# A gated linear attention feeding a squared-ReLU MLP: the instruction order planned anew, with other gates on the input transfers

## The chip, the cores and the metric

The kernel runs on one core of a Trainium2 chip. The metric is the device time of one execution in microseconds (us). Before the change the median of three runs is 176.64 us (176.60, 176.64, 176.91).

The engines have short names in the profile: PE multiplies matrices (PEld loads its stationary operand), DVE, ACT and POOL work on elements, SP issues transfers and does nothing else here. POOL issues transfers too. Each engine takes its own instructions strictly in order; engines wait for each other through semaphores.

## The reference

For each of 4 batches and 8 heads, a state of 48x48 runs over 768 tokens; the outputs of all heads of a token, 384 numbers, are a row x of a two-layer MLP:

```python
for t in range(S):
    state = alpha[:, :, t, :, None] * state + np.einsum('bhd,bhe->bhde', k[:, :, t], v[:, :, t])
    y[:, :, t] = np.einsum('bhd,bhde->bhe', q[:, :, t], state)
...
h = x @ w_in            # 384 -> 2048
r = np.maximum(h, 0.0)
return ((r * r) @ w_out).astype(np.float32)   # 2048 -> 384
```

Inputs and output are float32; 3072 rows of 384 come out.

## The kernel before

**Tiles.** The 3072 tokens are cut into 12 pieces of 256 tokens, called pairs here (g = 0 to 11; each is two chunks of 128, and three pairs make a batch). Each pair goes through these steps:

- `loads` (L497): four transfers issued by SP, alpha, k, q and v of the pair, 384 KB each, into one of four raw buffers. All loads of all pairs are kept in one order.
- `decay` (L519), or `decay_half` (L558) for pairs 0 and 1, which does it in two halves X of four heads: ACT takes logarithms (lab), PE sums them (L534, L536; L573, L578 for halves), ACT exponentiates (asb), DVE multiplies q and k by the result (qks; L555, L587). `values` (L511) makes a bf16 copy of v (vbf): on POOL for pairs 0 and 1 (L515), else on ACT (L517).
- the transposes of qks into qkt: on PE with eviction by ACT and DVE for pairs 0 to 3 (`turned`, L606 and L611; `turned_half`, L638, L649, L652), by a transposing DMA on SP from pair 4 on (`turned_dma`, L618).
- `scores` (L654): 64-wide matmuls (L666), then DVE applies the causal mask out of PSUM (pm, L676).
- `carry` (L682): the state to hand on (L695, then DVE L710/L713 and POOL L715).
- `mixed` (L723): the attention output of the pair, transposed as the MLP needs it (L734), copied by ACT into xt (L773). For pairs 6 to 10 `mixed_back` (L781) makes it token-major instead (L804, L794), ACT copies it into yb (L818), and a transposing DMA on SP (L821) makes xt.
- `up` (L838): 8 units of 6 matmuls 128x256 (L847) into psH0 and psH1 in turn, ReLU on ACT (rr, L853), square on DVE (gt, L855).
- `down` (L867): for each chunk 4 pieces of 4 matmuls 128x384 (L874) into psO, ACT copies out (osb, L881), then a store (L831) by SP, or by POOL in two halves for pairs 6 to 10. The last chunk is done in two column halves (L893, L900).

**Weights.** w_in comes in five pieces and w_out in four (`weights`, L474). POOL issues these transfers, which also cast to bf16. `RUNS` (L466) says after which load each run of pieces may start: (1, 3, 5) is five pieces after alpha of pair 1, (1, 2, 4) four pieces after v of pair 1. `OPENS` (L467) makes alpha of pair 2 wait for piece 5, the first of w_out.

**What sets the order.** Nothing is issued in program order of the source. Each step is recorded with a number `at` (pair index times two plus an offset, L904 to L931), its cost and its dependences; `Program.order` (L88) then plays list scheduling with assumed durations, transfer rates (L39 to L43) and instruction-fetch blocks (L47), picks for each engine the ready step with the smallest `at`, and so fixes each engine's instruction order. `fill` (L263) puts matmuls on zeros into planned idle time of PE ahead of the first `down`; `busy` (L859) issues seven such matmuls of 512 columns at the start. Nobody reads their output. `plan` and `emit` turn dependences into semaphore waits. So a constant or an offset changes the order of whole engines.

Of the kernel before, what the change touches and what calls it, by code (L numbers as in the profile page):

```python
# [14 lines left out]

class Op:


    def __init__(self, n, eng, fn, work, at, dma=None, nbytes=0, rate=0.0):
        self.n, self.eng, self.fn, self.work, self.at = n, eng, fn, work, at  # L20
        self.dma, self.nbytes, self.rate = dma, nbytes, rate
        self.deps = {}
        self.users = []
        self.waits = []
        self.count = None
        self.signal = False
        self.form = None
        self.size, self.late = 0, 0.0


class Program:
# [7 lines left out]
    BEGIN = {"SP": 1200.0, "POOL": 2700.0}  # L39
    LANDING = {"SP": 900.0, "POOL": 1400.0}  # L40
    PAIR, ROWS, TURN = 325.0, 390.0, 135.0
    PACKET = {PAIR: 120.0, TURN: 256.0}
    LONG = 1792.0  # L43
    HOLD = 2500.0
    SWITCH, STICK = 95.0, 1.0

    BLOCK, AHEAD_OF_ALL, FETCH, CALM, BUSY_UNTIL = 256, 37, 5200.0, 500.0, 36000.0  # L47
    FILL, SHARE, WIDE = 215.0, 0.75, 4

    def __init__(self, nc):  # L50
        self.nc = nc
        self.ops = []
        self.writer = {}
        self.readers = {}
        self.slots = {}

    def add(self, eng, fn, work, at, reads=(), writes=(), dma=None, nbytes=0, rate=0.0, behind=None, form=None,
            drain=None, size=0):
        op = Op(len(self.ops), eng, fn, work, at, dma, nbytes, rate)
        for r in reads:  # L60
# [23 lines left out]
        op.form, op.size = form, size  # L84
# [3 lines left out]
    def order(self, until):  # L88
        until = {op.n for op in until}
        missing = {}  # L90
        for op in self.ops:
            missing[op.n] = len(op.deps)
            for d in op.deps:
                self.ops[d].users.append(op)
# [11 lines left out]
        def done(op, t, users):  # L106
            for u in users:
                known[u.n] = max(known[u.n], t)
                missing[u.n] -= 1
                if not missing[u.n]:  # L110
# [3 lines left out]
        now = [0.0]  # L114

        def transfer(limit):

            while now[0] < limit:
                on = [e for e in queue if queue[e] and queue[e][0][0] <= now[0]]
                end = min([limit] + [queue[e][0][0] for e in queue if queue[e] and e not in on])  # L120
                if not on:
                    if end == limit:
# [3 lines left out]
                    continue  # L126
                rate = {}
                for e in on:
                    op = queue[e][0][2]
                    rate[e] = op.rate if len(on) == 1 else self.PACKET.get(op.rate, self.LONG) / sum(  # L130
                        self.PACKET.get(queue[o][0][2].rate, self.LONG) / queue[o][0][2].rate for o in on)
# [7 lines left out]
                if queue[first][0][1] <= 1e-3:  # L139
                    op = queue[first].pop(0)[2]  # L140
                    op.landed = op.landed0 = end + self.LANDING[first]
# [10 lines left out]
        for op in self.ops:  # L152
            if not missing[op.n]:
# [5 lines left out]
        used, there, filling = self.AHEAD_OF_ALL, {}, True  # L159
        while left:  # L160
# [37 lines left out]
            op = self.ops[n]  # L198
            if e == "PE":
                if op.form != form:  # L200
                    op.work += self.SWITCH
                form = op.form
                filling = filling and n not in until
                if filling and used > self.AHEAD_OF_ALL:
                    gap = 2 * int(max(0.0, t - free[e]) * self.SHARE / self.FILL)
                    used, there = self.take(used, gap, free[e], 100.0, there)[:2]
                used, there, late = self.take(used, op.size + 1, t, op.work, there)
                op.work += late
                op.late = late
            free[e] = t + op.work  # L210
            op.start = t
            programs[e].append(op)
            self.sequence.append(op)
            left -= 1
            if op.dma is not None:
                if e == "SP":
                    issued += 1
                    if op.rate == self.TURN:
                        turning[0] = op
                queue[e].append([t + self.BEGIN[e], float(op.nbytes), op])  # L220
                done(op, free[e], [u for u in op.users if u.eng == e and u.deps[n] == "order"])
            else:
                end = free[e] + self.LATENCY[e]
                if e == "PE":
                    done(op, free[e], [u for u in op.users if u.eng == e and u.deps[n] != "drain"])
                    done(op, end, [u for u in op.users if u.eng == e and u.deps[n] == "drain"])
                else:
                    done(op, free[e], [u for u in op.users if u.eng == e and u.deps[n] == "war"])
                    done(op, end, [u for u in op.users if u.eng == e and u.deps[n] != "war"])
                reserve = self.RESERVE if op.at > 4 else 0  # L230
                done(op, end + reserve, [u for u in op.users if u.eng != e])
        self.programs = programs

    def take(self, used, size, t, work, there):
# [3 lines left out]
        block = used // self.BLOCK  # L238
        for b in range(block + 1, (used + size) // self.BLOCK + 1):
            at = t + late + work * (b * self.BLOCK - used) / size  # L240
            late += max(0.0, there.get(b, 0.0) - at)
            there[b + 1] = max(at, there.get(b, 0.0)) + self.FETCH - (self.CALM if at > self.BUSY_UNTIL else 0.0)
# [87 lines left out]
def bass_gla_recurrent__then__act_relu_squared_kernel(  # L330
# [71 lines left out]
    turn = [0]  # L402

    def bank():
        i = turn[0] % len(psG)
        turn[0] += 1
        return psG[i], ("psG", i)
# [50 lines left out]
    BACK = 6  # L458
    TURNED = 4
    SELF = 12  # L460


    RUNS = [(1, 3, 5), (1, 2, 4)]
    OPENS = {2: 5}
# [9 lines left out]
    def weights(at, run):  # L474
        x0 = sum(r[2] for r in RUNS[:run])
        w0, j0, n0 = RUNS[run]
# [21 lines left out]
    def loads(g, at):  # L498
        b, t0, r = g // NW, (g % NW) * TW, g % NRAW
        for j, src in ((3, alpha), (0, k), (1, q), (2, v)):  # L500
# [3 lines left out]
            eng = "SP" if g < SELF else "POOL"  # L504
            last_load[0] = add(eng, lambda e, s=s, dst=dst: e.dma_start(dst, s), 500 if g < SELF else 1000, at + 0.1 * (j != 3),
                               writes=raw(r, j), reads=gate, dma=("raw" if g < SELF else "own") + f"{r}_{j}",
                               nbytes=TW * HD * 4, rate=pr.PAIR, behind=last_load[0])
            if g - 2 in turns and j == 3:
                last_load[0].deps.setdefault(turns[g - 2].n, "order")

    def values(g, at):  # L511
        r, vb = g % NRAW, g % NV
        dst, src = VBF[vb][:, :, :, 0:D], both(r, 2)
        if g < FIRST:
            add("POOL", lambda e: e.tensor_copy(dst, src), 910, at, reads=raw(r, 2), writes=[("vbf", vb)])  # L515
# [3 lines left out]
    def decay(g, at):  # L519
# [4 lines left out]
        def product(dst, at_, a0, a1, reads, writes):  # L524
            add("DVE", lambda e: e.tensor_tensor(dst, a0, a1, ALU.mult), 470, at_, reads=reads, writes=writes)  # L525
# [13 lines left out]
        add("PE", sums, 265, at + 0.02, reads=lab + ["hinc"], writes=[key], size=2 + 2 * NP)  # L539
# [13 lines left out]
        for z in range(2):  # L553
# [4 lines left out]
                writes=[("qks", x, z, X) for X in range(2)])  # L558
        values(g, at + 0.3)

    def decay_half(g, X, at):

        r, l, a, x, c_ = g % NRAW, g % NLAB, g % NASB, g % NQK, g % NAC
        ps, key = bank()
# [5 lines left out]
        def sums(pe):  # L570
            for o in range(2):
                for i in range(2):
                    pe.matmul(ps[:, o * HH:(o + 1) * HH], (HEXC if i == 1 and o == 0 else HINC)[:],  # L573
                              LAB[l][:, i, hs, 0:D], start=i == 0, stop=i == 1)
            for j in range(2):
                for i in range(2):
                    h = 4 * X + 2 * j
                    last = pe.matmul(ps[:, HD + 2 * j:HD + 2 * j + 2],  # L578
                                     LAB[l][:, i, h:h + 2, :].rearrange("p a b -> p (a b)"),
                                     HINC[:, 63:128:64], start=i == 0, stop=i == 1)  # L580
            return last
        add("PE", sums, 430, at + 0.01, reads=[("lab", l, X), "hinc", "hexc"], writes=[key], size=16)
# [409 lines left out]
```

## Time and profile before

| what | value |
|---|---|
| median of three runs | 176.64 us |
| span of the profiled execution, first to last instruction | 175.4 us |
| the rest of a run, median less span | 1.2 us |
| PE, DVE, ACT, POOL busy | 169.2, 120.3, 115.4, 31.3 us |
| first `up` matmul starts | 19.07 us |
| first `up` matmul of pair 2 starts | 47.06 us |
| HBM read, written | 25.17 MB, 4.72 MB |

The profile is of one execution; its own time outside the span is not recorded, so 1.2 us is taken for it. The page gives busy times, the chain of work that ended last, the groups of instructions by source line and the transfers; the views of windows, waits and single tiles are answers of the same trace. L numbers are lines of the kernel before. Times inside the execution count from the first instruction.

### The profile page before, as it was taken

What the parts mean: (1) busy time and instruction counts of PE and PEld (TensorE: products, weight loads), DVE (VectorE), ACT (ScalarE), POOL (GpSimd) and SP (SyncE); (2) the same over time, 40 slices, a digit from 0 to 9 for tenths busy, and PEclk for the clock granted to TensorE, in tenths of its full rate; (3) what the DMA queues carried; (4) which work ended last, traced back from release to release, by engine and by line L of the source; (5) the groups of instructions that cost most, each with busy time, mean ns of one, the idle gap of its engine ahead of it and who ended that gap; (6) DMA issues with size and microseconds to landing.
All of it is one profiled execution on the core that took longest, in us unless ns stands there. A gap on an engine that the chain in (4) does not pass through costs nothing.

```text
span 175.4 us, 5998 instructions
## 1 busy us (share of the span) xinstructions
PE 169.2 (96%) x2614; PEld 123.4 (70%) x2614; DVE 120.3 (69%) x253; ACT 115.4 (66%) x235; POOL 31.3 (18%) x56
## 2 busy tenths in 40 slices
PE   7987999999999999999999999999999999999994
PEld 2554777775777678777776776776787777777773
DVE  7799643689989898957949749759749527322320
ACT  2763565895798598778749659658665563476541
POOL 4189110001011012010020010212222221220120
PEclk9999999999999999999999999999999999999999
DMA  5999999999997999998999996999639622202222
GB/s 143 325 298 174 204 203 251 255 317 308 331 244 145 273 222 262 216 265 267 117 319 191 185 327 113 176 331 124 122 76 78 135 49 45 49 0 49 47 45 90
DMA packets 77818, 32.30 MB, mean 184 GB/s; under 512 B 71264, under 2 KB 77472, under 8 KB 77792
## 3 DMA queue, kind: packets, MB, share of 16 engines
q1 hardware_dynamic: 72720, 26.81, 67.1%
q0 software_dynamic: 5072, 5.11, 16.9%
q8 instruction: 20, 0.33, 0.8%
q14 instruction: 6, 0.05, 0.1%
HBM read 25.17 MB, written 4.72 MB: 170 GB/s over the span
## 4 chain that ended last, share of the span: by engine, by line
PE 93%; DVE 4%; ACT 1%; issue 1%
PE psH L847 37%; PE psO L874 35%; PE psG L734 5%; PE psG L666 4%; PE psO L862 3%; DVE qks L587 3%; PE psG L695 2%; PE psO L893 2%; PE psG L804 1%; PE psG L606 1%; DVE pm L676 1%; PE psG L794 1%; PE psG L534 1%; PE psG L573 1%; ACT xt L773 1%
## 5 line engine op out<-in xcount | busy, mean ns | idle before, releaser
L853 ACT ACTIVATE rr<-psH 128x512 bf16<-128x512 f32 x96 | 57.0, 600 | 35.3 <-PE psH L847 34.2
L847 PE MATMUL psH<-xt,win 128*128 128x256 bf16 x576 | 75.3, 273 | 0.1
L874 PE MATMUL psO<-wout,gt 128*128 128x384 bf16 x368 | 73.3, 326 | 0.0
L855 DVE TENSOR_TENSOR gt<-rr 128x512 bf16<-128x512 bf16 x96 | 40.7, 428 | 40.8 <-ACT rr L853 40.4
L847 PEld LDWEIGHTS psH<-xt,win 128*128 128x128 bf16 x576 | 54.9, 98 | 13.7 <-ACT xt L773 0.4
L874 PEld LDWEIGHTS psO<-wout,gt 128*128 128x128 bf16 x368 | 34.2, 98 | 15.6
L676 DVE TENSOR_TENSOR pm<-psG,mask 128x512 bf16<-128x512 f32 x48 | 30.4, 681 | 0.7 <-PE psG L666 0.7
L715 POOL TENSOR_TENSOR sbf<-ust,acp 128x192 bf16<-128x192 f32 x16 | 10.0, 626 | 86.0 <-DVE ust L713 86.0
L555 DVE TENSOR_TENSOR qks<-raw,asb 128x768 bf16<-128x768 f32 x20 | 18.5, 952 | 0.8 <-ACT asb L544 0.8
L831 POOL DMA_DIRECT2D out_dram<-osb x20 | 10.8, 544 | 44.3 <-ACT osb L881 44.3
L881 ACT ACTIVATE osb<-psO 128x384 f32<-128x384 f32 x23 | 11.3, 490 | 5.0 <-PE psO L874 4.5
L525 DVE TENSOR_TENSOR raw<-raw 128x384 f32<-128x384 f32 x20 | 11.5, 581 | 0.0
L544 ACT ACTIVATE asb<-psG 128x384 bf16<-128x384 f32 x20 | 9.9, 493 | 0.5 <-PE psG L536 0.4
L773 ACT ACTIVATE xt<-psG 128x384 bf16<-128x384 f32 x14 | 7.6, 600 | 3.1 <-PE psG L734 3.1
L517 ACT ACTIVATE vbf<-raw 128x768 bf16<-128x768 f32 x10 | 8.6, 860 | 0.0
L862 PE MATMUL psO<-warm 128*128 128x512 bf16 x20 | 7.5, 498 | 1.1 <-DVE warm L420 1.1
L666 PEld LDWEIGHTS psG<-qkt 64*64 64x64 bf16 x384 | 5.9, 106 | 3.5 <-issue 1.9
L666 PE MATMUL psG<-qkt 64*64 64x128 bf16 x384 | 8.3, 219 | 0.0
L713 DVE TENSOR_TENSOR ust<-psG,sbf 128x192 f32<-128x192 f32 x15 | 5.3, 355 | 3.4 <-PE psG L695 1.7
L818 ACT ACTIVATE yb<-psG 128x384 bf16<-128x384 f32 x10 | 4.6, 489 | 3.9 <-PE psG L794 3.0
L734 PEld LDWEIGHTS psG<-pm,vbf 64*64 64x64 bf16 x336 | 4.9, 107 | 2.0 <-DVE pm L676 0.6
L530 ACT ACTIVATE lab<-raw 128x384 bf16<-128x384 f32 x10 | 5.3, 529 | 1.4 <-DVE raw L525 1.3
(71 smaller groups left out, 123.4 us busy)
## 6 DMA issues: line engine op xcount, KB each, us to landing
raw<-in_alpha_dram SPq DMA_DIRECT2D x12, 384.0 KB, 4.5
raw<-in_k_dram SPq DMA_DIRECT2D x12, 384.0 KB, 5.0
raw<-in_q_dram SPq DMA_DIRECT2D x12, 384.0 KB, 5.2
raw<-in_v_dram SPq DMA_DIRECT2D x12, 384.0 KB, 5.9
out_dram<-osb SPq DMA_DIRECT2D x13, 192.0 KB, 4.9
out_dram<-osb POOLq DMA_DIRECT2D x20, 96.0 KB, 2.3
wout<-in_moe_w_out_dram POOLq DMA_DIRECT2D x4, 384.0 KB, 11.8
win<-in_moe_w_in_dram POOLq DMA_DIRECT2D x3, 384.0 KB, 8.5
```

Of the source, the lines that this page charges most:

```text
L525: add("DVE", lambda e: e.tensor_tensor(dst, a0, a1, ALU.mult), 470, at_, reads=reads, writes=writes)
L555: add("DVE", lambda dve, z=z, decays=decays: dve.tensor_tensor(QKS[x][:, z, :, :, 0:D], both(r, z), decays, ALU.mult), 870, at + 0.05 + 0. ...
L666: last = pe.matmul(banks[i, j // 2][0][64 * c:64 * c + 64, col:col + 128].rearrange("p (a b) -> p a b", a=2), QKT[t][64 * i:64 * i + 64, 0 ...
L676: add("DVE", lambda dve, i=i, X=X, ps=ps: dve.tensor_tensor(PMB[m][:, i, 2 * X:2 * X + 2].rearrange("p j n s -> p j (n s)"), ps[:].rearran ...
L734: last = pe.matmul(o, lhsT, rhs, start=(c, n % 2) not in begun, stop=True, skip_group_check=True)
L831: add(by, lambda e, dst=dst, ps=ps: e.dma_start(dst, OSB[o][ps, :]), 600, at + 0.01 * i, reads=[("osb", o)], dma=("own" if by == "POOL" el ...
L847: last = pe.matmul(ps[:, f * TW:(f + 1) * TW].rearrange("p (c t) -> p c t", c=2), WIN[:, kt, fj * 128:(fj + 1) * 128], XT[:, 2 * (g % NX): ...
L853: add("ACT", lambda act: act.activation(RR[r][:], ps[:], AF.Relu), 480, at, reads=[key], writes=[key, ("rr", r)])
L855: add("DVE", lambda dve: dve.tensor_tensor(gt[:, 2 * u:2 * u + 2, :], rr, rr, ALU.mult), 340, at, reads=[("rr", r)], writes=[("gt", g % NG ...
L862: last = pe.matmul(psO[i % NPO][:, 0:128 * wide].rearrange("p (a b) -> p a b", a=wide), WARM[:], bass.AP(tensor=WARM, offset=0, ap=[[128, ...
L874: last = pe.matmul(ps[:, 0:DM], GT[g % NGT][:, fj, tt * 128:(tt + 1) * 128], WOUT[:, fj, :], start=(fj == 0), stop=(fj == FT - 1))
L881: add("ACT", lambda act: act.activation(OSB[o][:], ps[:, 0:DM], AF.Copy), 372, at, reads=[key], writes=[key, ("osb", o)])
```

## The change

The planner and its numbers are replaced; what is computed stays. In the built program:

- **Order.** A table with offsets for each pair and step replaces four shared rows of offsets, and the planner's assumptions on rates, fetch blocks (254 instructions for 256), the cold start of PE and the SBUF port shared by DVE and POOL change. Every engine's order changes. On PE, pair 0 now goes through scores, carry and the first 48 matmuls of `mixed` ahead of the transposes of pair 1; before, the transposes and half of the scores of pair 1 came first.
- **v of pairs 0 and 1.** The POOL copy also waits for all of that pair's qks.
- **Weights.** Eight pieces follow alpha of pair 1 and the ninth v of pair 1 (`PARTS`), so POOL's copy of v of pair 1 comes after eight pieces and the first state multiply, not after five.
- **Loads.** Alpha of pair 2 waits for piece 6 (second of w_out), alpha of pair 3 for piece 7. The loads of pairs 4 and 5 stand ahead of the first store in SP's queue. Only pairs 10 and 11 still wait for an earlier transpose to be issued (9 and 8); before, every pair from 6 on waited for that of two pairs earlier.
- **y by tokens** (`mixed_back`) for pairs 7 to 10; pair 6 goes by `mixed`, its rows stored by SP.
- **The sums** for the state (128x2 matmuls) of pairs 0 and 1 are all done with the second half: 4 and 12 matmuls for the halves, where 8 and 8 stood.
- **The start.** 14 matmuls of 256 columns for 7 of 512; later fillers write psO1 alone. In all 25 fillers for 20.
- **PSUM banks** go by least recent use, and pairs 0 and 1 may use psH and psO0 too.

```diff
-    RUNS = [(1, 3, 5), (1, 2, 4)]
-    OPENS = {2: 5}
+PARTS = ((1, 3, 8), (1, 2, 1))
+OPENS = {2: 6, 3: 7}
-    BACK = 6
+BACK = (7, 8, 9, 10)
+BEHIND = {10: 9, 11: 8}
+WARMUP = (14, 2)
...
-    BLOCK, AHEAD_OF_ALL, FETCH, CALM, BUSY_UNTIL = 256, 37, 5200.0, 500.0, 36000.0
+    BLOCK, AHEAD_OF_ALL, FETCH, CALM, BUSY_FROM, BUSY_UNTIL = 254, 56.0, 6500.0, 2000.0, 11200.0, 31000.0
...
+TABLE = [
+    dict(decay0=-98.35796, decay1=-86.77717, turned0=-92.08415, turned1=-74.82202, scores0=-76.59803, scores1=-74.23854, carry=-69.28206, mixed=-45.90118, up=-40.7555, down=13.8692, ...
...
-            if g - 2 in turns and j == 3:
-                last_load[0].deps.setdefault(turns[g - 2].n, "order")
+            if g in BEHIND and j == 3:
+                last_load[0].deps.setdefault(turns[BEHIND[g]].n, "order")
...
         if g < FIRST:
-            add("POOL", lambda e: e.tensor_copy(dst, src), 910, at, reads=raw(r, 2), writes=[("vbf", vb)])
+            add("POOL", lambda e: e.tensor_copy(dst, src), 830, at,
+                reads=raw(r, 2) + [("qks", g % NQK, z, X) for z in range(2) for X in range(2)], writes=[("vbf", vb)], port=True)
...
-            for j in range(2):
-                for i in range(2):
-                    h = 4 * X + 2 * j
-                    last = pe.matmul(ps[:, HD + 2 * j:HD + 2 * j + 2],
...
+            for j in range(2 * NP * X):
+                h, i = j // 2 * 2, j % 2
+                last = pe.matmul(ps[:, HD + h:HD + h + 2],
...
     def turned_back(g):
-        return BACK <= g < G - 1
+        return g in BACK
...
-    add("PE", lambda pe: busy(pe, 7, 4), 2950, -6, reads=["warm"], writes=[("psO", i) for i in range(NPO)], size=14)
+    add("PE", lambda pe: busy(pe, WARMUP[0], WARMUP[1]), 2950, -6, reads=["warm"], writes=[("psO", 1)], size=2 * WARMUP[0],
+        cold=False)
```

More of the change, by code (lines that the diff above doesn't have):

```diff
@@ L159, in order @@
         used, there, filling = self.AHEAD_OF_ALL, {}, True
+        port = {"DVE": 0.0, "POOL": 0.0}
+        other = {"DVE": "POOL", "POOL": "DVE"}
         while left:
@@ L197, in order @@
             n = pick[1]
[L198 to L209, printed above, removed]
@@ L699, in mm @@
             return last
-        add("PE", mm, 170 + 150 * len(chunks), at, reads=[("qks", x, 0, X) for X in range(2)] + [("vbf", vb)],
+        add("PE", mm, 250, at, reads=[("qks", x, 0, X) for X in range(2)] + [("vbf", vb)],
             writes=[b[1] for b in banks], form=64, size=32 * len(chunks))
```

385 lines of the change are left out of this document (272 added, 113 removed).

## Prediction

> **What bounds the kernel now.** I read the chain of waits first, then the busy time by stretch, then the timelines of the start, then the landing times. From the page and the stretches:
>
> ```profile
> PE 93%; DVE 4%; ACT 1%; issue 1%
> 27.14:47.06 19.92, 19.92 (x272) 14.38 (x270) 15.66 (x30) 14.13 (x31) 0.75 (x1) 1.00 1.10 293
> 47.06:110.00 62.94, 62.94 (x1083) 46.76 (x1081) 51.94 (x104) 49.31 (x103) 5.46 (x8) 1.00 1.01 226
> 110.00:173.00 63.00, 62.98 (x869) 47.25 (x867) 32.51 (x68) 36.36 (x70) 12.78 (x24) 1.00 0.51 94
> ```
>
> The columns are length of the stretch, then busy time of PE, PEld, DVE, ACT, POOL, the granted clock and the transfers. From 27.14 to 173 us PE is busy all the time: no wait there to remove. The change can win only ahead of 27.14, by less PE work, or not at all; it can lose anywhere. Two views of the start:
>
> ```profile
> 16.99 0.83 PE psG L734 x48
> 17.84 1.18 ACT xt L773 x2
> 19.07 1.48 PE psH L847 x12
> 26.65 0.65 PE psO L874 x4
> ```
>
> This is the chain: first `up` unit at 19.07, after the copies of xt, after `mixed` of pair 0.
>
> ```profile
> 8.07 0.82 POOL L515 CAST vbf<-raw 128x768 bf16<-128x768 f32 x1 [4.51 <-DMA raw<-in_v_dram]
> 9.41 4.00 POOL L481 DMA_DIRECT2D win<-in_moe_w_in_dram  x5 [0.53 <-DMA raw<-in_alpha_dram]
> 13.42 0.84 POOL L515 CAST vbf<-raw 128x768 bf16<-128x768 f32 x1
> 14.19 3.00 POOL L483 DMA_DIRECT2D wout<-in_moe_w_out_dram  x4
> 12.77 2.84 DVE L587 TENSOR_TENSOR qks<-raw,asb 128x384 bf16<-128x384 f32 x4
> ```
>
> A qks product takes 0.55 us, one following another every 0.47; but four took 2.84 us from 12.77 (one of them 1.44) and one at 8.12 took 1.18, each beside a POOL copy of v.
>
> The landing times, asked piece by piece: the last two pieces of w_in
>
> ```profile
> DMA to landing us min/median/max: 8.5/8.5/8.5
> DMA to landing us min/median/max: 9.6/9.6/9.6
> ```
>
> issued at 11.88 and 12.65, so landed at 20.4 and 22.2; the piece before landed at 18.45. w_out lands at 24.15, 26.2, 28.1 and 30.95. One piece takes 1.9 us in the stream; the last took 2.9 beside pair 2's loads, of which alpha is issued at 24.16, on the landing of piece 5.
>
> **The change, part by part.**
>
> 1. *Pair 0 first: the first `up` unit.* Alpha and k land as before, so the first qks product starts at 6.3 (before 6.42). The copy of v now waits for all four, so they run at 0.47: done 8.3 (before 9.30). Two qkt copies of 0.41 on DVE: 9.25. Four masks, one every 0.60 from 9.2: done 11.7 (before 12.86). Four products of pair 1, no copy beside them: 11.6 to 13.6 (before 12.77 to 15.61). `mixed` of pair 0 no longer stands behind pair 1's transposes: its 48 matmuls (0.70) at 11.75. The rest needs sbf (0.34 on DVE, 13.9), six matmuls (0.15), the second transposes (0.45), six more: ends 14.9. One xt copy of 0.60, the other chunk's was done early: **first `up` at 15.7**, 3.4 earlier.
>
> 2. *The weights hold it.* Piece 1 of w_in is needed at 15.7 (landed 13.7), the second at 16.4 (lands 16.55), the third lands at 18.45, the fourth at 20.4. POOL's first issue stays at 9.41, for alpha of pair 1 lands at 9.12 and the copy of v, started 8.4, ends 9.25. So units 0 and 1 are done with 0.75 us to spare, units 2 and 3 run 18.5 to 19.8, half of pair 1's scores 0.33, unit 4 waits for 20.4. From there: units 4 and 5 1.4, `mixed` of pair 1 0.95, unit 6 0.75, twelve matmuls 0.29, unit 7 0.65, one `down` 0.65: 25.1. Before, the same work was done at 27.14: **-2.05**. Of 3.4 won, 1.35 is lost to the weights.
>
> 3. *To the first `up` of pair 2 (47.06 before).* xt of pair 1 is copied by 25.1; eight units (5.24) and three `down` pieces (1.95): 32.4, each later than its w_out piece. Then twelve `down` pieces (7.8), pair 2's transposes, carry and scores, sums of pairs 2 and 3 and the changes of tile shape (2.7): `mixed` of pair 2 at 42.9 to 44.1. The new order has used up every `down` of pair 1 by then; before, one stood between `mixed` and this `up`, another inside `mixed`. What is late next: the sums of pair 3 (PE 41.9), two exps (0.49 each, a logarithm between them), two products of 0.95 end at 44.9, its transposes at 45.4; two xt copies of 0.60 behind 44.3 and ACT's other work end at 45.6. `up` at 45.7: **-1.36**, so 0.7 is given back.
>
> 4. *The rest.* Unit, piece and changes of shape are the same number (29 episodes of 64-wide work behind the first `up` in both orders). Pair 6 costs 0.70 + 0.27 + 0.29 by `mixed` (pair 3's row) for 0.85 by `mixed_back` (88.36 to 89.48 less a carry of 0.27): **+0.25**, for +0.4 at most. It saves SP one transpose of y.
>
> Costed at nothing: the 14 narrow matmuls (same 3584 columns, and the sums wait for ACT's logarithm at 4.90 anyway); the regrouped sums (0.1 earlier for the first half, 0.2 later for the second, inside the 0.75 of step 2); banks; planner numbers without effect on the order. If the 0.75 is used up, the start costs one for one.
>
> *POOL's copies, moved.* The copy of v of pair 0 now falls beside qkt copies and masks. Beside a mask, POOL's multiply at 17.18 (0.55) and the masks (0.68, as elsewhere) cost each other nothing; beside a qks product the copy cost 0.63. Between 0 and +0.63 I take 0, since the copies read PSUM as the masks do; the spare 0.75 covers the other end. The Trainium skill, "SBUF — State Buffer", section "Who interferes with whom", says that a DVE instruction with two SBUF inputs and a GpSimd one that reads SBUF exclude each other for a whole instruction, and that one with at most one SBUF input outside its two-port modes does not contend; by it the cost is 0 too. The 1.18 and 1.44 for 0.55 agree with its first half; no run yet shows a copy out of PSUM beside the cast.
>
> *Pair 2 let in late.* Its alpha is issued at 26.2 for 24.16. Its lateness is between 0 and 2.0. I take 0 for the last load: pieces 7 and 8 of the weights keep the queues full until then (DMA slices of 9), so alpha merely shares later, and v of pair 2 landed at 35.2 behind the same bytes. Alpha is then there at 31.4; its product, logarithm and sums are wanted at 34.4. The Trainium skill, "DMA: Bandwidth & Descriptors", in its part on software and hardware descriptor generation, says that an engine goes round-robin between the queues and changes at packet boundaries; by it a late alpha takes its share from the last piece alone, which ends near 31 as before. That piece's 2.9 us beside the loads agrees.
>
> *The DMA transposes.*
>
> ```profile
> DMA to landing us min/median/max: 4.2/5.5/6.1
> DMA to landing us min/median/max: 2.8/4.5/5.3
> ```
>
> The first line is for qkt, the second for xt. SP issues the first 3.0 to 4.6 us after PE's sums (48.38 to 52.99, 92.10 to 95.63). So scores need 7.2 to 10.7 us after the sums. With PE full from 45.7, I added up the new order by rows (a unit 0.655, a `down` piece 0.65, the rest as above): it leaves 15, 14, 11.3, 16, 16, 18, 11.3 and 12 us for pairs 4 to 11. Pair 6 is the tightest, 0.6 of room, since a store and a load of k stand ahead of it. For y of pairs 7 to 10 it leaves 8, 9, 6 and 6 us from ACT's copy, against up to 5.3, and more where a qkt transpose is still ahead in the queue. Taken as 0; between 0 and +1.
>
> **Sum**: 175.4 - 2.05 + 0.7 + 0.25 = 174.3 of span; with 1.2 outside it **175.5 us**, against the median 176.64.
>
> **Rivals.**
>
> - *Transposes late* (steps 4's cover fails at pair 6 and at y of 7 or 10): two waits of 0.4 to 0.6 each, 176.5. For: SP takes its list strictly in order, and five stores and loads now wait there between two transposes. Against: the room worked out above.
> - *Slower: the loads of pairs 2 and 3 shift by the whole 2.0 us.* Then alpha of pair 3 lands at 39.0 for 37.0. On DVE its product now stands between the two qkt copies of pair 2, and ACT's logarithm of pair 4's alpha between pair 3's two exps. PE has no `up` left to put in: scores of pair 2, due at 39.3, come at 40.3, and pair 3's transposes another 1.0 later. +2.0: 177.5. It decides once alpha of pair 3 lands after 38. Against it: bytes, not issue, set those landings before.
> - *It does not give back*: the transposes of pair 3 and xt of pair 2 are ready when PE is, at 45.0: 174.8; with w_out and w_in landing 0.4 earlier, because POOL issues eight pieces without a copy between, 174.4.
> - *The early start comes to nothing*: the copy of v of pair 0 and PSUM banks borrowed from psH and psO hold pair 0 past 0.75 of spare; 176.6, no change.
>
> **Chances.** Forecast 0.50 (own range 175.0 to 176.2), transposes late 0.17, loads late 0.15, no giving back 0.12, no early start 0.06. A measurement of this kernel can tell about 0.2% (0.35 us) from no change. Faster by more: 0.50 less 0.02, and 0.12, and 0.06 of the transposes' case: 0.66. Within: 0.16, mostly late transposes and no early start. Slower: 0.18 (late loads and the worse half of late transposes). The range takes in the case without giving back and the loads' case: 174.3 to 177.5; below lies what the weights forbid, above it several waits at once.
>
> **What will show it.** First `up` near 15.7, the fifth unit at 20.4 right behind the landing of its piece, the first `down` done at 25.1, `up` of pair 2 near 45.7, PE busy without a gap from there to the end, end of span at 174.3. No qks product of pairs 0 and 1 over 0.6 us. Wrong if weights land at other times than before, if scores of pair 2 or 3 wait on a load, or if scores of pair 6 or the first units of pairs 7 to 10 wait on SP's transposes.

## The result, and the profile after

The changed kernel is **slower** by 0.8%: 178.63 us (median of 11 runs, 177.39 to 180.03) against 177.07 for the kernel before (11 runs, 176.60 to 178.85). The ratio is 1.0084, with a 95% interval of 1.0057 to 1.0111. On another chip it was 1.0053 (1.0018 to 1.0087). The forecast was 175.5. The ratios here and below compare fast executions alone, and one can differ by up to 0.4% from the quotient of the two medians.

The profiled execution took 178.44 us with a span of 176.2, so 2.2 us lie outside the span. The executions of the changed order have 2.17 to 2.29 us there (all but one variant, the last experiment), those of the kernel before 1.68 to 1.81. The 1.2 us of the prediction was too small for either: it set the median of three executions, which with 1.75 us outside would have a span of 174.9, against the 175.4 of another execution. As a span 175.4 is usual: the medians on five chips are 174.9 to 175.5.

The shares of the chain that ended last:

```profile
PE 71%; DMA 13%; SPq 9%; POOL 3%; ACT 1%; DVE 1%; issue 1%; DVEq 0%
```

It was 93% PE before. Now PE comes into it only at 49.33 us; ahead of that it runs mostly through transfers and SP's issuing. The first `up` units, which the change brought forward, do not stand in it. Its middle part:

```profile
13.50 0.74 POOL wout L574
14.27 11.80 DMA wout<-in_moe_w_out_dram
...
40.37 1.15 SPq L595
41.56 6.35 DMA raw<-in_v_dram
```

The second piece of w_out lands at 26.08. Alpha of pair 2 waits for it by the new gate (a gate here is the wait of a load for a piece of the weights). Then come eleven issues of SP, one behind the other, and last the load of v of pair 4. The chain does not say that an earlier gate brings this load forward by as much: in the profile before, alpha of pair 2 was issued 1.93 us earlier, and v of pair 4 only 0.47 (41.09). Next three stretches, from the first `down` done, from the first `up` of pair 2 (both the same work as in the prediction's table) and from 110 us:

```profile
24.90:45.65 20.75, 20.13 (x272) 14.49 (x271) 15.43 (x29) 14.97 (x32) 0.76 (x1) 1.00 1.08 262
45.65:110.00 64.35, 62.74 (x1095) 46.91 (x1093) 51.78 (x104) 48.21 (x100) 4.92 (x8) 1.00 0.97 227
110.00:173.80 63.80, 63.78 (x870) 47.41 (x868) 32.27 (x68) 37.83 (x72) 10.96 (x20) 1.00 0.45 98
```

PE (second figure) was busy through all three before. Now the first lacks 0.6 us, the part that the prediction saw given back, and the middle one 1.6. The chain goes on there:

```profile
47.92 0.02 issue
47.94 0.84 ACT vbf L608
48.78 0.50 ACT rr L958
49.28 0.05 issue
49.33 1.49 PE psH L952 x12
```

The load of v of pair 4 lands at 47.92. ACT copies it (L608 of the changed kernel) and only then does the ReLU `rr` (L958) that frees psH for PE's third `up` unit of pair 2. The copy itself is wanted by nobody before `carry` of pair 4 at 58.6. ACT's timeline (start, duration, operation, idle time before it in brackets):

```profile
45.29 0.54 ACT L638 ACTIVATE ro<-ro 128x384 f32<-128x384 f32 x1
47.94 0.84 ACT L608 ACTIVATE vbf<-raw 128x768 bf16<-128x768 f32 x1 [2.11 <-DMA raw<-in_v_dram]
48.69 1.07 ACT L958 ACTIVATE rr<-psH 128x512 bf16<-128x512 f32 x2
```

The planner put the copy in line ahead of the ReLU; by its own times it would start at 46.0. In the kernel before, ACT does the first two ReLUs of pair 2 ahead of the copy:

```profile
47.92 1.25 ACT L853 ACTIVATE rr<-psH 128x512 bf16<-128x512 f32 x2
49.07 0.48 ACT L544 ACTIVATE asb<-psG 128x384 bf16<-128x384 f32 x1
49.44 0.84 ACT L517 ACTIVATE vbf<-raw 128x768 bf16<-128x768 f32 x1
```

DVE stands in the same way, under the cover of ACT's wait:

```profile
46.65 0.55 DVE L616 TENSOR_TENSOR raw<-raw,ro 128x384 f32<-128x384 f32 x1
49.06 0.56 DVE L616 TENSOR_TENSOR raw<-raw 128x384 f32<-128x384 f32 x1 [1.87 <-DMA raw<-in_alpha_dram]
49.54 0.75 DVE L960 TENSOR_TENSOR gt<-rr 128x512 bf16<-128x512 bf16 x2
```

This product belongs to pair 5, whose alpha lands at 49.04; behind it wait the squares gt of pair 2. In the kernel before, this product stands behind the fourth gt.

At the start all went as forecast in this execution. DVE and POOL:

```profile
6.81 1.50 DVE L680 TENSOR_TENSOR qks<-raw,asb 128x384 bf16<-128x384 f32 x3 [0.18 <-DMA raw<-in_q_dram]
8.33 0.42 DVE L745 COPY qkt<-psH 128x512 bf16<-128x512 bf16 x1
8.80 0.42 DVE L745 COPY qkt<-psG 128x512 bf16<-128x512 bf16 x1
9.16 0.69 DVE L769 TENSOR_TENSOR pm<-psG,mask 128x512 bf16<-128x512 f32 x1
```

```profile
8.38 0.82 POOL L605 CAST vbf<-raw 128x768 bf16<-128x768 f32 x1 [4.81 <-DVE qks L680]
```

Three products take 0.50 each; beside POOL's cast (8.38 to 9.20) two qkt copies take 0.42 each, as they do alone. The first mask starts at 9.16 and so hardly meets the cast.

### The profile page after: what moved, and what is told of

Its sections match the earlier page's. It is cut to its first block, busy times and chain, and to the rows that moved or that the text cites. A ratio compares the mean times of both kernels' runs of the same rounds, so it can differ in the third digit from the quotient of the medians.

```text
span 176.2 us, 6026 instructions
## 1 busy us (share of the span) xinstructions
PE 168.7 (96%) x2631; PEld 123.7 (70%) x2631; DVE 118.7 (67%) x253; ACT 116.8 (66%) x233; POOL 28.9 (16%) x52
## 4 chain that ended last, share of the span: by engine, by line
PE 71%; DMA 13%; SPq 9%; POOL 3%; ACT 1%; DVE 1%; issue 1%; DVEq 0%
PE psH L952 30%; PE psO L981 29%; SPq L595 9%; DMA wout<-in_moe_w_out_dram 7%; DMA raw<-in_v_dram 4%; PE psG L827 3%; PE psG L759 3%; DMA raw<-in_q_dram 3%; POOL win L572 2%; PE psO L1000 2%; PE psG L788 1%; PE psG L909 1%; PE psG L899 1%; DVE qks L680 1%; PE psG L626 1%
## 5 line engine op out<-in xcount | busy, mean ns | idle before, releaser
L958 ACT ACTIVATE rr<-psH 128x512 bf16<-128x512 f32 x96 | 57.2, 601 | 30.3 <-PE psH L952 29.1
L952 PE MATMUL psH<-xt,win 128*128 128x256 bf16 x576 | 74.1, 273 | 1.7 <-ACT rr L958 1.6
L981 PE MATMUL psO<-wout,gt 128*128 128x384 bf16 x368 | 71.2, 326 | 0.0
L769 DVE TENSOR_TENSOR pm<-psG,mask 128x512 bf16<-128x512 f32 x46 | 29.6, 683 | 4.1 <-PE psG L759 4.1
L938 POOL DMA_DIRECT2D out_dram<-osb x16 | 8.6, 540 | 29.6 <-ACT osb L988 29.4
L608 ACT ACTIVATE vbf<-raw 128x768 bf16<-128x768 f32 x10 | 8.5, 849 | 4.5 <-DMA raw<-in_v_dram 4.4
L868 ACT ACTIVATE xt<-psG 128x384 bf16<-128x384 f32 x13 | 7.0, 599 | 2.4 <-PE psG L827 2.4
L967 PE MATMUL psO<-warm 128*128 128x256 bf16 (+1 forms) x25 | 6.4, 393 | 1.1 <-DVE warm L516 1.1
L827 PE MATMUL psG<-pm,vbf 64*64 64x128 bf16 x312 | 6.0, 218 | 0.1
L616 DVE TENSOR_TENSOR raw<-raw,ro 128x384 f32<-128x384 f32 x10 | 5.5, 549 | 0.0
```

The lines of the kernel that those rows point to most:

```text
L769: add("DVE", lambda dve, i=i, X=X, ps=ps: dve.tensor_tensor(PMB[m][:, i, 2 * X:2 * X + 2].rearrange("p j n s -> p j (n s)"), ps[:].rearran ...
L827: last = pe.matmul(o, lhsT, rhs, start=(c, n % 2) not in begun, stop=True, skip_group_check=True)
L952: last = pe.matmul(ps[:, f * TW:(f + 1) * TW].rearrange("p (c t) -> p c t", c=2), WIN[:, kt, fj * 128:(fj + 1) * 128], XT[:, 2 * (g % NX): ...
L958: add("ACT", lambda act: act.activation(RR[r][:], ps[:], AF.Relu), 480, at, reads=[key], writes=[key, ("rr", r)])
L981: last = pe.matmul(ps[:, 0:DM], GT[g % NGT][:, fj, tt * 128:(tt + 1) * 128], WOUT[:, fj, :], start=(fj == 0), stop=(fj == FT - 1))
```

## The experiments

Medians, ratio to the kernel before (run on the same chip beside it; it had 176.59 to 177.22 there), the median of the spans of all executions, and time less span:

| run | median us | ratio, 95% | span | outside |
|---|---|---|---|---|
| changed kernel | 178.63 | 1.0084 (1.0057 to 1.0111) | 176.4 | 2.2 |
| e0_before | 177.06 | 1.0013 (0.9978 to 1.0048) | 175.3 | 1.7 |
| e1_v4_later | 177.56 | 1.0056 (1.0026 to 1.0087) | 175.3 | 2.2 |
| e2_v3_v4_later | 178.16 | 1.0089 (1.0053 to 1.0125) | 176.0 | 2.2 |
| e3_gate_piece5 | 176.84 | 1.0018 (0.9983 to 1.0054) | 174.6 | 2.2 |
| e4_v4_a5_later | 177.96 | 1.0049 (1.0015 to 1.0084) | 175.8 | 2.2 |
| e5_v4_a5_gate5 | 177.39 | 1.0056 (1.0021 to 1.0090) | 175.2 | 2.2 |
| e6_all_gate5 | 177.35 | 1.0024 (0.9995 to 1.0053) | 175.1 | 2.2 |
| e7_before_no_clash | 175.92 | 0.9938 (0.9905 to 0.9972) | 174.2 | 1.8 |
| e8_all_spread | 176.71 | 1.0026 (0.9990 to 1.0061) | 174.5 | 2.2 |
| e9_before_early | 178.12 | 1.0102 (1.0052 to 1.0152) | 176.4 | 1.7 |
| e10_seven_wide | 177.54 | 1.0069 (1.0032 to 1.0106) | 175.3 | 2.2 |
| e11_after_clash | 178.18 | 1.0100 (1.0049 to 1.0151) | 176.0 | 2.2 |
| e12_pool_longer | 176.07 | 0.9982 (0.9956 to 1.0007) | 174.3 | 1.7 |
| e13_dve_longer | 176.73 | 1.0010 (0.9974 to 1.0046) | 174.5 | 2.2 |
| e14_no_clash_again | 175.94 | 0.9969 (0.9941 to 0.9997) | 174.3 | 1.7 |
| e15_spread_no_gate | 177.50 | 1.0029 (0.9994 to 1.0065) | 175.3 | 2.2 |
| e16_gate_again | 177.11 | 1.0026 (0.9995 to 1.0057) | 174.9 | 2.2 |
| e17_after_again | 177.63 | 1.0053 (1.0018 to 1.0087) | 175.4 | 2.2 |

A single execution varies by 2 us or more, mostly with the landing of the loads, so the profile of a run shows what waits for what, and the medians what it costs. The gaps of PE given below run from the end of its steady stream of matmuls and are 0.1 to 0.2 us longer than those in the view of waits, which takes the modelled end of the last matmul (1.6 there for the 1.69 us at 47.64 in the profile after).

### The kernel before, once more (e0_before)

> The kernel before, unchanged, to have spans and times of one kernel side by side. Theory (the 1.2 us outside the span was wrong because the profiled execution was slower than the median): time less span is 2.2 us in each execution, median 177.1, typical span 174.9, and executions range by over 1 us. Rival (the kernel before has less time outside its span than the changed one): 1.2 us.

Time outside the span was 1.7, so the rival's 1.2 was as wrong as the theory's 2.2. The second profile (span 174.2) shows more. DVE's products of pairs 0 and 1:

```profile
6.04 1.96 DVE L587 TENSOR_TENSOR qks<-raw,asb 128x384 bf16<-128x384 f32 x4 [0.29 <-ACT asb L584]
11.55 1.97 DVE L587 TENSOR_TENSOR qks<-raw,asb 128x384 bf16<-128x384 f32 x4
```

No product is slow. They began 0.38 us earlier than in the first profile and were done at 8.00, before POOL's cast at 8.01. First `up` at 16.96 instead of 19.07. Of the 3.4 us that the prediction won there, 2.1 are won in this execution of the kernel before, with nothing changed; at the first `up` of pair 2 it is 1.5 us ahead of the first profile (45.56 for 47.06). And in this execution v of pair 4 landed at 48.15, later than in the changed kernel, without a wait of PE: ACT did the ReLUs at 46.41 and the copy at 48.17.

### The clash taken out of the kernel before (e7_before_no_clash, e14_no_clash_again)

The clash is POOL's copy of v falling on DVE's qks products, as in the first profile.

```diff
 values(g), g = 0, 1: POOL tensor_copy vbf<-raw, order kept
-    waits for v of the pair
+    waits for v of the pair and for its four qks products on DVE
```

> The kernel before with one thing added: POOL's copies of v of pairs 0 and 1 wait until the four qks products of their pair are done, the order kept. A second profile of the kernel before had no copy beside a product, its first up at 16.96 instead of 19.07, and its times lie in two groups, 175.2 to 176.4 (12 of 35) and 176.9 to 178.0 (22 of 35). Theory (the groups are executions without and with the clash, so the 3.4 us that the prediction won at the first up was there to win in some executions only): the upper group goes, median 175.9, ratio 0.993 to 0.995, first up near 17.0. Rival (the weights hold units 4 to 8 in either case, or the groups come from later loads): both groups stay, median within 0.4 us of 177.1.

> The kernel before with POOL's copies held back, once more, on the chip of the two runs beside it. If the changed order is worth nothing beyond the clash: 0.3 us or more under whichever of the two has 1.75 us outside the span, or the same. If the changed order is worth something of its own: that one is faster by 0.2 us or more.

175.92 and 175.94, first `up` at 16.96 and 17.58. Most executions now have spans of 173.5 to 174.7 (9 of 12 and 10 of 12). The theory holds: this one wait is worth 0.3 to 0.6%, and the kernel before with it alone beats both the kernel before and the changed one. It also equals the changed kernel with the moves, the earlier gate and the longer POOL program of the experiments below, run beside it on one chip (e12: 176.07, median span 174.3, for 175.94 and 174.3 here). By the terms set for e14, the changed order is worth nothing that shows beyond the clash.

### The copy of v of pair 4 moved back (e1_v4_later, e2_v3_v4_later)

```diff
 ACT, up of pair 2:
-copy of v of pair 4
 rr, rr, asb, lab, rr, asb, rr
+copy of v of pair 4
 (e2 also: copy of v of pair 3 behind the logarithm ahead of that copy)
```

> The changed kernel with its planned order kept, but ACT's copy of v of pair 4 (0.84 us) put behind the fourth square of up of pair 2 instead of ahead of the first. Theory (ACT works in order, and this copy's wait for v of pair 4, landed 47.92, holds the squares behind it, so that PE's third unit of pair 2 waits 1.69 us): the wait goes, the span falls from 176.2 to about 174.5, the time to about 176.9 us, a ratio of 0.999 to before. Rival 1 (v of pair 4 is only the first of several late things, the next wait takes its place): the time falls by less than 0.6 us, ratio 1.005 or more. Rival 2 (the loss is not in this wait but spread, or outside the span): no change, 1.008.

> As the run before, and ACT's copy of v of pair 3, which waited 1.96 us for its landing at 41.55, goes behind the work that stood between it and pair 4's copy. Theory (the same in-order wait also makes the exps of pair 3 late, and through them PE's gaps of 0.31 and 0.51 us at the transposes of pair 3): a further 0.3 to 0.8 us, span 173.7 to 174.2, time near 176.2, ratio 0.995. Rival (these gaps come from the sums of pair 3 and from DVE, as the prediction had it): the same as the run before within 0.2 us.

The first has 1.0056 where the changed kernel has 1.0084, and 1.0053 on another chip; the intervals overlap, so that moving the one copy gains anything is not shown. In its profile the wait of ACT is gone and DVE is next in line:

```profile
49.30 0.56 DVE L616 TENSOR_TENSOR raw<-raw 128x384 f32<-128x384 f32 x1 [1.56 <-DMA raw<-in_alpha_dram]
49.77 0.75 DVE L960 TENSOR_TENSOR gt<-rr 128x512 bf16<-128x512 bf16 x2
```

PE waited 1.07 us for gt. Rival 1 is right about the ratio (not about the time, 1.07 us less), and the cause is of the same kind. The second run gained nothing more (1.0089): in its profile, of an unusually long execution, PE's gaps at the transposes of pair 3 stayed (0.40 and 0.51), so its theory fails.

### Both moved back, and the gate (e3_gate_piece5, e4_v4_a5_later, e5_v4_a5_gate5, e6_all_gate5)

```diff
 ACT, up of pair 2:   copy of v of pair 4 as above, and behind it
+lab (logarithm of alpha of pair 5)
 DVE, up of pair 2:
-product of alpha of pair 5
 gt, gt, qks, gt
+product of alpha of pair 5
 alpha of pair 2 waits for (e3, e5, e6):
-    piece 6 of the weights (lands 26.1)
+    piece 5 (24.1)
 (e6 also: the moves of pair 4 told below)
```

> The changed kernel with its planned order kept; only the load of alpha of pair 2 waits for the piece of w_out that lands at 24.12 instead of the next, at 26.08. Theory (the bytes ahead of them set when the loads of pairs 3 and 4 land, not the gate): v of pair 4 lands within 0.7 us of 47.9, PE still waits over 1 us, the time within 0.5 us of 178.6. Rival (the late gate makes v of pair 4 late): it lands near 46.4 as before the change, the wait of 1.69 falls to about 0.2 us, span 174.7, time 177.1, ratio 1.000.

> The changed kernel, planned order kept, with ACT's copy of v of pair 4 and ACT's logarithm of alpha of pair 5 behind the fourth square of up of pair 2, and DVE's first product of alpha of pair 5 behind the third gt of up of pair 2. In the run that moved only the copy, PE waited 1.07 us for gt, and DVE stood at that product, whose alpha landed at 49.27. Theory (two engines wait in order for two late loads, one behind the other; together they hold PE for 1.7 us): PE has no wait over 0.3 us from 46 to 56, spans 1.4 to 1.7 us under the changed kernel's 176.4, near 174.8, time near 177.0, ratio 0.999. Rival (a third operation waits for a load and takes their place): 0.5 us or less below the 177.56 of the run with the copy alone is not reached, time 177.3 or more.

> The run before plus the earlier gate (alpha of pair 2 waits for the landing at 24.1 instead of 26.1). Theory of orders (once nothing waits in line for a late load, the gate is worth nothing): the same as the run before within 0.3 us. Rival (the gate moves the loads of pairs 2 to 5 earlier by 1 us or more, and pairs 2 and 3 gain from it too): 0.5 us or more faster than the run before, below 176.5.

> The run before plus DVE's first product of alpha of pair 4 behind the two qks products of pair 3, ACT's logarithm of it behind the copies of xt of pair 2, and DVE's product of q of pair 4 behind the second gt of up of pair 2. Theory (DVE's 0.3 to 0.4 us of waiting for alpha of pair 4 reaches PE at the transposes of pair 3, where PE's gap is 0.3 to 0.5): that gap falls by 0.3 us, time 0.3 us under the run before. Rival (DVE's own 1.8 us of products set it, or the sums of pair 4 come late instead): no change within 0.2 us, or slower.

Without the gate (e4) the rival came true: a third operation took the place of the two. ACT's line:

```profile
51.95 0.62 ACT L958 ACTIVATE rr<-psH 128x512 bf16<-128x512 f32 x1
54.90 0.84 ACT L608 ACTIVATE vbf<-raw 128x768 bf16<-128x768 f32 x1 [2.33 <-DMA raw<-in_v_dram]
55.65 1.07 ACT L958 ACTIVATE rr<-psH 128x512 bf16<-128x512 f32 x2
```

That is the copy of v of pair 5, again ahead of ReLUs of pair 2; PE waited 1.91 us. The gate alone (e3) came near its rival: 176.84 and 1.0018, v of pair 4 landed at 46.90 and ACT began its copy at 47.03 without waiting. Added to the moves (e5) it gave 0.6 us by the medians and nothing by the ratios (1.0056 for 1.0049), so these runs don't decide. In e6 the gap at the transposes of pair 3 was 0.33 against 0.38: the rival, DVE's own work sets it. What e6 has left is 0.22, 0.56 and 0.24 us where three moved operations stand in a row on ACT.

### All moves, spread (e8_all_spread), without the gate (e15_spread_no_gate), the gate alone and the changed kernel on one chip (e16_gate_again, e17_after_again)

```diff
 ACT, up of pair 2:
 rr x6
+lab of pair 5
 rr x2
+copies of v of pairs 4 and 5
 (each taken from its planned place; product of alpha of pair 5 as above,
 lab of pair 4 behind the copies of xt of pair 2)
 DVE: product of alpha of pair 4 behind the qks of pair 3, of q of pair 4 behind the second gt
```

> The changed kernel with all the moves of the run with everything, but ACT's copies of v of pairs 4 and 5 behind the last square of up of pair 2 and its logarithm of alpha of pair 5 behind the sixth (in that run three operations stood in a row behind the fourth, and PE had gaps of 0.22, 0.56 and 0.24 there; in the run with the gate of before ACT waited 2.33 us for v of pair 5 in the same place). Theory (what is left of the loss inside the span is these gaps, 1.0 us, and 0.3 by mixed of pair 6): spans near 174.0, a microsecond under that run, time near 176.3, ratio 0.995. Rival (ACT is simply full there, and the squares come late in any order): 177.0 or more.

> The run with all moves spread, but with the changed kernel's late gate. That run (176.71, ratio 1.0026, spans around 174.5) and the one with the earlier gate alone (176.84, 1.0018, 174.6) came out alike, so the runs so far don't tell which of the two it takes. Theory of places (operations that wait in line for loads): spans around 174.5, time 176.7, whatever the gate. Theory of the gate (it makes the loads of pairs 2 to 5 late, and the places matter little): spans of 175.5 or more, 177.7.

> The run with the earlier gate alone, once more, on the chip of the two runs beside it. Theory of places: the gate takes away only a part of the wait, spans 0.5 to 1.5 us under those of the changed kernel, and the profile still shows ACT or DVE waiting for v of pair 4 or alpha of pair 5. Theory of the gate: spans around 174.6 and no such wait.

> The changed kernel itself on this chip: 178.6 us, spans around 176.4, PE waiting 1 to 2 us between 47 and 50, behind the copy of v of pair 4.

With all moves and the gate, spans come to 174.1 (four of twelve) and 174.5 in the median; the prediction's sum said 174.3, for an order without this wait. The time that the theory gave, 176.3, was missed by 0.4 us, which is the 0.5 by which the spans missed its 174.0. The ratio 0.995 was further off: it went by 177.07 for the kernel before, which had 176.59 on this chip. The changed kernel itself had 177.63 on the last chip, 1.0 less than expected, but its profile shows the same wait, behind v of pair 4 landing at 48.38:

```profile
48.41 0.84 ACT L608 ACTIVATE vbf<-raw 128x768 bf16<-128x768 f32 x1 [1.49 <-DMA raw<-in_v_dram]
49.16 1.07 ACT L958 ACTIVATE rr<-psH 128x512 bf16<-128x512 f32 x2
```

Moves alone and gate alone (1.0029 and 1.0026 beside 1.0053) can't be told apart there, nor, by the intervals, from the changed kernel. In the traces of the changed order v of pair 4 lands at 45.4 to 50.2 with the late gate (mean of eight 47.65; 47.2 without the two longest executions, e2 and e15) and at 45.5 to 46.9 with the earlier one (mean of seven 46.15). So there the gate moves the load by some 1.0 to 1.5 us. But in the five traces of the kernel before and its variants, whose gate is the earlier piece, the load lands at 46.4 to 48.2 (mean 47.48), about as late as in the changed kernel, and PE waits for it in none where the copy stands behind two ReLUs. So the place in line decides whether a late landing hurts. The same wait also turns up later: in the profile of e15, another long execution, ACT waited 1.48 us for v of pair 7, again ahead of a ReLU, and PE had four gaps of 0.4 to 0.8 from 60 to 82 us, the first of them behind ACT's wait of 1.33 for alpha of pair 6.

### The places in line alone, in the kernel before (e9_before_early)

```diff
 kernel before, without the clash; ACT and DVE, up of pair 2:
+copy of v of pair 4            +product of alpha of pair 5
 rr, rr, asb                     gt, gt, qks, gt, ..., gt, ..., qks
-copy of v of pair 4            -product of alpha of pair 5
```

> The kernel before without the clash (median 175.92 beside 177.04), with two operations put where the changed kernel has them: ACT's copy of v of pair 4 ahead of the first square of up of pair 2, two squares earlier than before, and DVE's first product of alpha of pair 5 ahead of the first gt, four earlier. No load and no PE instruction is moved. Theory (the place in line is the loss): PE waits 1.0 to 2.5 us after the first units of pair 2, time 177.0 to 178.4, ratio 1.000 to 1.008. Rival (the loss needs the later loads of the changed kernel): 176.2 or less, 0.995.

178.12, against 175.92 and 175.94 for the same kernel without the two moves on other chips: +2.2, or 1.3 to 1.6% by the ratios. The time lies where the theory had it, the ratio of 1.0102 above. The waits from 44 to 54 us (total, times, longest):

```profile
DVE raw L525 <- DMA raw<-in_alpha_dram: 2.7, 1, 2.7
...
PE psH L847 <- ACT rr L853: 1.6, 1, 1.6
ACT vbf L517 <- DMA raw<-in_v_dram: 1.1, 1, 1.1
```

No load, gate or PE instruction was touched, and v of pair 4 landed at 47.90, where the other traces of this order have it. This shows that the place in line is enough.

### The other edits (e10_seven_wide, e11_after_clash)

```diff
-busy(pe, 14, 2)
+busy(pe, 7, 4)
```

> The changed kernel with the seven 512-column unread matmuls of before in place of the fourteen of 256. All runs of the kernel before have 1.69 to 1.80 us outside the span, all of the changed one 2.17 to 2.29. Theory (this edit costs nothing inside the span, as predicted, and has no part in the 0.45 us outside it): time 178.4 within 0.5, 2.2 us outside. Rival (PE's first instructions set what lies outside the span): 1.75 us outside.

> The changed kernel, order kept, with POOL's copies of v of pairs 0 and 1 no longer waiting for the qks products (pair 1's copy still stands behind all but one of the weight issues, after its products). Theory (the products of pair 0 come 0.2 to 1.2 us later in some executions; the weights hold units 2 to 4 anyway, so little of it reaches the first down): time 178.6 to 179.0, first up up to 1 us later, first down at most 0.4 later. Rival (the wait is what the change wins by, even beside the weights): 179.3 or more.

In e11 POOL's copies no longer wait for the qks products. Neither differs from the changed kernel beyond the intervals; the first `up` was at 16.14 and 15.92. So the 14 matmuls show no cost, as forecast, and no part in the time outside the span (2.2 us without them too); e10's time was 0.9 us under what its theory gave. The wait of POOL shows no worth in the new order, but e11 tells little: it has six executions, and in its profile the products were not slowed (0.50 each).

### The time outside the span (e12_pool_longer, e13_dve_longer)

```diff
 POOL at 100 us (e12), or DVE at 161 us (e13), in the order of e8:
+memset(pad[:, i:i + 1], 0.0)   for i in range(8), read by nobody
```

> The run with all moves spread, plus eight memsets of one unused column each on POOL at about 112 us, where it is idle for 11 us. In every trace of the kernel before, six fetches of 8,192 bytes of instructions lie in the span, the last at 162 to 164; in every one of the changed kernel five do, and a sixth comes 1.0 us behind the end of the span. POOL has 73 recorded instructions before and 68 after the change, DVE 284 and 278. Theory POOL (POOL's program became shorter, so that its last block of code is fetched after the end, which costs the 0.45 us outside the span): 1.75 us outside, median near 176.2. Theory DVE or neither: 2.2 us outside, median 176.7.

> The run with all moves spread, plus eight memsets of one unused column each on DVE at about 161 us, where it is idle for 3 us. Theory DVE (DVE's program is the one that became shorter than its last block): the sixth fetch moves into the span, 1.75 us outside it, median near 176.2. Theory POOL or neither: 2.2 us outside, 176.7.

Eight useless instructions on POOL make the kernel 0.66 us faster than on DVE (176.07, 176.73, one chip), with 1.69 to 1.79 us outside the span instead of 2.17 to 2.28. The queue of instruction fetches of the page, for the changed kernel and for e12 (packets, MB, share):

```profile
q14 instruction: 5, 0.04, 0.1%
```

```profile
q14 instruction: 6, 0.05, 0.1%
```

In the packet records the sixth fetch of 8,192 bytes starts 1.0 to 1.2 us behind the end of the span in all fourteen traces of the changed kernel and its variants but e12, where it comes at 149.9; in the kernel before and its variants it comes at 161.6 to 164.5. Theory POOL holds: the length of POOL's program, four DMA issues shorter by the change, decides whether the sixth fetch falls into the span or behind it, and the latter goes with 0.45 us more outside. That the program ended just ahead of a block of code is the reading that fits.

## Why the prediction was wrong

The chance given to "slower" was 0.18, and the rival behind it was another mechanism. The step that failed is the fourth, PE dense from the first `up` of pair 2 to the end. By steps, in the one profile after:

1. **First `up`**: 15.7 forecast, 15.99 measured; products, copies and masks within 0.1 us. Right, with some luck: in the fifteen traces of the changed order and its variants it lies from 15.79 to 17.40.
2. **Weights hold it**: first `down` done at 24.90 (25.1). Right. The fourth piece of w_in landed at 19.75 (20.4 forecast), unit 4 started at 19.88.
3. **Pair 2**: 45.65 (45.7). Right for the profile; the fifteen traces have 45.01 to 47.56. The Trainium skill, "DMA: Bandwidth & Descriptors", section "Queues, rings and completion order", lets queues take turns by packet; by that rule, alpha of pair 2, issued 1.9 us later, would lose little: it landed at 31.20 (31.55 before), and the trace agrees. But for v of pair 2 the prediction took 0 as well; it came 1.04 later (36.24 for 35.20), and loads behind it by up to 1.5.
4. **The rest, dense to the end**: this is the step that failed. +0.26 for pair 6 is right (1.38 us for 1.12), though the +0.25 was a choice below the 0.4 that the prediction's own rows give; and PE waited for no transposing transfer. But PE lost 1.69 us at 47.64. The prediction asked of each load when PE wanted what is made of it, and found the answer far away. It didn't ask what stands behind the first user of the load on that user's engine. Of ACT's copy PE needed nothing until 58.6; the ReLUs behind it held PE at once. The runs show in its place: this wait in two profiles of the changed kernel (1.69 us at 47.64 here, again on the last chip), and +2.2 us by the two places alone in the kernel before (e9).

The sum with measured terms: 175.4 - 2.24 + 0.83 + 0.26 + 1.69 + 0.26 (small gaps) = 176.2, where the small gaps are what is left over. Forecast was 174.3.

Two terms lay outside the sum. **The base**: the 2.05 us at the start were worked out against an execution with the clash of POOL's copy and DVE's products. Its span was usual; by the spans about a third of the executions go without the clash. Profiles without it (e0_before, e7, e14) have the first `up` of pair 2 at 45.1 to 45.6, where the changed kernel has it. Against those the start wins nothing, and the clash alone, where it happens, is what the change could win: the order of pair 0, to which the prediction's first step gave part of the 3.4 us, shows no worth of its own by then. **Outside the span**: +0.45 by POOL's code, nowhere in the sum and not to be read from a trace of before; and 1.75 for 1.2 in the kernel before.

Of the rivals, "loads late" came nearest: alpha of pair 3 landed at 37.30 and did no harm, but v of pair 4 harmed through ACT's line. It was 1.5 us later than in the first profile before, though only 0.4 later than the mean of the five traces of that order. The rival's point of decision was the wrong one.

On the clash, the Trainium skill, "SBUF — State Buffer", section "Who interferes with whom", says that a DVE instruction with at most one SBUF input doesn't contend with GpSimd outside its two-port modes. What no run showed at the prediction, the trace after now shows, and agrees: 0.42 us for a copy out of PSUM beside the cast, as alone.

What stays open is how the loss inside the span divides between gate and places (together 1.0 us by the ratios 1.0084 and 1.0026, 1.9 by the spans 176.4 and 174.5, 0.5 by the ratios on the last chip, where the median spans, 175.4 and 175.2 before, differ by 0.2 alone), and what makes loads land as unevenly as they do.

## What to carry to other kernels

For each engine, list what stands in line ahead of the work PE will ask for next, and which of it waits for a transfer: an operation that nobody needs for 10 us can hold PE by its place alone, and taking one away shows the next. Before a stall in one profile is booked as a gain, look in how many executions it is: a second profile of the kernel before had none of it, and by the spans a third of all executions have none. And compare times with spans: what lies outside the span differs between programs.

## What the runs showed of the hardware

- In the two profiles of the kernel before, a difference of 0.4 us in the start of DVE's products decided whether POOL's copy fell on them; with it the first `up` moved by 2.1 us; with the wait added, 19 of 24 spans of that kernel lie from 173.5 to 174.7, without it a third (52 of 149).
- A program of POOL that is shorter by a few instructions can be slower: 0.45 us with a fetch of code behind the end, gone with eight memsets.
- Two of the late landings in the profile after (v of pair 2, 2.58 us behind q; v of pair 4, 2.26) coincide with fetches of 16,384 bytes of instructions at 33.54 and 44.97, which took 1.30 and 0.92 us; most loads of this trace follow each other by 1.0 to 1.3, a few others by 1.6 to 2.0. No run tried to move these fetches, so that they delay the loads is only argued.
